# One batch's attention interleaved by priority, and VectorE's small steps with PSUM operands or an accumulator

## The chip, the cores and the metric

The kernel runs on one core of one Trainium2 chip. The metric is the time of one execution on the device in microseconds (us), the median over several runs. TensorE (PE) multiplies, PEld is its loading of weights, DVE is VectorE, ACT is ScalarE, POOL is GpSimd; SP issues the transfers. Each engine takes its own queue of instructions in order; an instruction may wait for semaphores of the others.

## The reference

Eight batches of S = 576 tokens. Three layers follow one another.

```python
a = exp(phi - phi.max(2)); a = a / (a.sum(2) + 1e-9)          # over the tokens, M = 32 memory slots
k_m = einsum('bhsm,bhsd->bhmd', a, k); v_m = einsum('bhsm,bhsd->bhmd', a, v)
x = softmax(q @ k_m.T / 8) @ v_m                               # 8 heads of 64: x is 576 x 512
u = x + (x.T @ U @ V).T                                        # rank 32, over the tokens
y = u + relu(u @ w_ch1) @ w_ch2                                # 512 -> 2048 -> 512
# then four experts, the two with the largest logits y @ w_gate kept for each token:
p = softmax(causal(y @ wq[e] @ (y @ wk[e]).T / 8)); out += w[e] * (p @ (y @ wv[e])) @ wo[e]
```

## The kernel before, in words

Every product is made from halves: a float32 operand is scaled by a power of two and split into a high and a low float16 part, and three matmuls (high·high, high·low, low·high) replace one in float32. The power of two comes from the largest absolute value of the operand. That largest value lies in one column, a number for each partition; to spread it over all partitions, `diagonals` (L236 to L242) writes a diagonal matrix of it (bfloat16, identity times the column, L241, tile `dg`, for the large weights `dgw`), `over_rows` (L244) multiplies that by ones on TensorE into a PSUM tile, a reduction on VectorE takes the maximum of each row, and `scales` (L253 to L259) makes the two powers of two from it with three steps on VectorE.

`stage1(b)` is the attention to the memory and the rank-32 mix. It reads phi and the raw q, k, v in four pairs of heads. For each pair: `pair_max` (absolute maxima; for batch 1 on ScalarE, L598), `pair_scale` (L612 and `scales`), `pair_hl` (splits to `kvq`, the low halves on GpSimd, L636, or VectorE, L639), `pair_kv` (36 matmuls `kv`, L656), `pair_kb`, `pair_scores` (18 matmuls `ss`, L683 to L685, and the transposition `vt`), then the softmax: `soft_a` (L783, L785) and `soft_b` (sum L795, then L797, the reciprocal L799, and the multiplication on GpSimd at L804 into `at`). For two pairs together `half_t` (transposing DMA to `aT`), `half_p` (`tu`, L826), `half_tt` (`tt`, L834), `half_tx` (`tx`, L846) and `half_u` (`u`, L873, L878) follow, then `u_max`, `u_scale` and `u_split` (`uhl`, L973, L975).

`mlp(b)` is 768 matmuls in four rounds: 8 `up` of 12 matmuls (`up`, L999; ScalarE L1003 and VectorE L1005 split the result to `h`) and 4 `down` in two parts of 12 (`dn`, L1015; VectorE adds into `u` at L1022). `stage2(b)` is the experts: `y_split` (L1093, L1095), `proj` (`pj`), `vg`, `gate`, `unit_s` (scores `sc` and softmax, `pT` by a transposing DMA), `unit_v` (`av` in PSUM, L1299), `unit_o` (L1306: denominators on ScalarE; L1308 reciprocal, L1310 times the gate's weight into `fac`; then ScalarE L1335 scales `av` to `ohl`) and `unit_w` (`wo`, output).

The first part of the program, `run(True)`, holds the conversion of w1 and w2 (`w1_conv`, `w2_conv`, `w1_split`, `w2_split`; L266 to L326; long steps of 128x1024 elements on ScalarE, VectorE and GpSimd), stage 1 of batch 0, the MLP of batch 0 and stage 1 of batch 1. The second, the loop, holds for b = 1 to 6 the MLP of b, stage 2 of b−1 and stage 1 of b+1. The last part takes the MLP of batch 7 and two stage 2 in an order written out by hand (`ORDER2`).

The order of the instructions: `at(t, step)` puts a step at a time in units, `run` traces the steps by that time, and a scheduler then orders each engine's queue by the trace order as priority, by its own estimate of when operands are ready. In the first part, the instructions of a step with `fill=True` are moreover held behind the last instruction, on each engine, of the recorded steps with a time up to the step's own less a slack; steps without it are recorded. PSUM has eight banks: tags `m` (3), `a` (4) and `v` (1, the `av` of the loop).

Of the kernel before, what the change touches and what calls it, by code (L numbers as in the profile page):

```python
# [46 lines left out]
START, SLACK, SLACK2, LATER = 53, 1.5, 4, 8  # L47
# [1509 lines left out]
```

## Time and profile before

| | |
|---|---|
| median of 3 runs | 1375.76 us (1375.38 to 1377.32) |
| the profiled execution | 1374.29 us, its span 1372.2 us |
| PE busy | 1240.5 us, 90% of the span |
| DVE busy | 962.7 us, 70% |
| ACT busy | 785.1 us, 57% |
| POOL busy | 406.7 us, 30% |
| granted TensorE clock, mean | 0.966 of full speed |

The numbers below PE are shares over the whole span; the stages have different limits, and the rows further down cut the span at the joints of the stages. The span leaves out 2.09 us of the execution's time. The loop from about 245 to 1270 us is three quarters of the span.

### The profile page before, as it was taken

What the parts mean: (1) busy time and instruction counts of PE and PEld (TensorE: products, weight loads), DVE (VectorE), ACT (ScalarE), POOL (GpSimd) and SP (SyncE); (2) the same over time, 40 slices, a digit from 0 to 9 for tenths busy, and PEclk for the clock granted to TensorE, in tenths of its full rate; (3) what the DMA queues carried; (4) which work ended last, traced back from release to release, by engine and by line L of the source; (5) the groups of instructions that cost most, each with busy time, mean ns of one, the idle gap of its engine ahead of it and who ended that gap; (6) DMA issues with size and microseconds to landing.
All of it is one profiled execution on the core that took longest, in us unless ns stands there. A gap on an engine that the chain in (4) does not pass through costs nothing. (4 is left out here: it accounts for less than half of the span.)

```text
span 1372.2 us, 31039 instructions
## 1 busy us (share of the span) xinstructions
PE 1240.5 (90%) x11932; PEld 950.0 (69%) x11932; DVE 962.7 (70%) x2673; ACT 785.1 (57%) x1886; POOL 406.7 (30%) x379
## 2 busy tenths in 40 slices
PE   5676895999989999989999999998998999999987
PEld 4454683777767777767767677676777777787764
DVE  7799866886678676776676766777667765644565
ACT  3786633666556555655564574565556556534476
POOL 3656512242321322232331322333222223001121
PEclk9789996999999999999999999999999999999998
DMA  9753320053422433143422433234232322201235
GB/s 255 207 171 93 82 66 18 20 109 63 94 53 54 95 76 71 38 96 72 79 62 52 86 70 73 57 75 96 50 75 57 79 58 53 58 14 35 41 81 112
DMA packets 257156, 106.40 MB, mean 78 GB/s; under 512 B 203792, under 2 KB 248528, under 8 KB 257008
## 3 DMA queue, kind: packets, MB, share of 16 engines
q1 hardware_dynamic: 257008, 104.43, 33.9%
q8 instruction: 93, 1.52, 0.4%
q14 instruction: 55, 0.45, 0.1%
HBM read 52.21 MB, written 9.44 MB: 45 GB/s over the span
## 5 line engine op out<-in xcount | busy, mean ns | idle before, releaser
L999 PE MATMUL up<-uhl,w1s 128*128 128x288 f16 x3072 | 429.6, 293 | 41.7 <-DVE h L1005 36.3
L1015 PE MATMUL dn<-h,w2s 128*128 128x288 f16 x3072 | 411.4, 287 | 6.4 <-DVE h L1005 4.3
L999 PEld LDWEIGHTS <-w1s 128*128 128x128 f16 x3072 | 301.2, 100 | 144.7 <-issue 60.9
L1015 PEld LDWEIGHTS <-w2s 128*128 128x128 f16 x3072 | 294.7, 98 | 86.8 <-issue 7.5
L1238 POOL TENSOR_TENSOR phl<-pr,phl 128x128 f16<-128x128 f32 (+3 forms) x112 | 92.5, 826 | 323.5 <-ACT phl L1236 235.3
L1005 DVE SCALAR_TENSOR_TENSOR h<-up,h 128x288 f16<-128x288 f32 x256 | 113.0, 450 | 84.0 <-ACT h L1003 83.1
L1003 ACT ACTIVATE h<-up 128x288 f16<-128x288 f32 x256 | 100.5, 401 | 87.7 <-PE up L999 85.4
L1235 ACT ACTIVATE pr<-sc,nm 128x128 f32<-128x128 f32 (+3 forms) x112 | 58.7, 524 | 122.3 <-DVE nm L1229 66.2
L636 POOL TENSOR_TENSOR kvq<-raw,kvq 96x768 f16<-96x768 f32 x48 | 78.4, 1652 | 145.9 <-ACT raw L630 139.8
L600 DVE TENSOR_REDUCE amax<-raw 96x1 f32<-96x768 f32 x72 | 68.1, 946 | 68.1 <-DMA raw<-in_v_dram 31.7
L1022 DVE SCALAR_TENSOR_TENSOR u<-dn,us,u 128x288 f32<-128x288 f32 x128 | 65.1, 509 | 33.0 <-PE dn L1015 32.4
L1299 PE MATMUL av<-vhl,pT 128*128 128x64 f16 (+1 forms) x1260 | 68.2, 195 | 14.7 <-DMA pT<-phl 13.3
L1299 PEld LDWEIGHTS <-pT 128*128 128x128 f16 (+1 forms) x1260 | 56.6, 102 | 35.7 <-DMA pT<-phl 17.9
L1229 DVE CUSTOM_DVE_ANT_0 sc<-sc,wmask,ysc 128x128 f32<-128x128 f32 (+3 forms) x128 | 69.3, 550 | 11.9 <-PE sc L1226 10.9
L624 ACT ACTIVATE kvq<-raw,ps 96x768 f16<-96x768 f32 x72 | 62.5, 924 | 6.6 <-DVE ps L257 6.5
L1236 ACT ACTIVATE phl<-pr 128x128 f16<-128x128 f32 (+3 forms) x112 | 52.2, 466 | 13.9 <-DMA pT<-phl 12.0
L1335 ACT ACTIVATE ohl<-av,fac 128x64 f16<-128x64 f32 (+1 forms) x140 | 35.7, 307 | 42.3 <-PE av L1299 33.2
L1356 PE MATMUL wo<-wos,oT 128*128 128x512 f16 (+1 forms) x288 | 57.0, 347 | 1.2 <-ACT oT L1328 0.7
L1153 PE MATMUL vg<-wvg,yhl 128*128 128x260 f16 (+1 forms) x504 | 49.2, 256 | 0.0
L1105 PE MATMUL pj<-yhl,wqs 128*128 128x288 f16 x336 | 47.4, 290 | 0.7 <-ACT u L881 0.7
L1120 ACT ACTIVATE qst<-pj 64x288 f16<-64x288 f32 x56 | 22.6, 404 | 42.7 <-PE pj L1105 42.3
L1105 PE MATMUL pj<-yhl,wks 128*128 128x288 f16 x336 | 46.6, 286 | 0.0
(317 smaller groups left out, 2291.2 us busy)
## 6 DMA issues: line engine op xcount, KB each, us to landing
w1s<-in_moe_w_ch_dram SPq DMA_DIRECT2D x32, 256.0 KB, 4.3
w2r<-in_moe_w_ch_dram SPq DMA_DIRECT2D x8, 1024.0 KB, 5.3
out_dram<-ob SPq DMA_DIRECT2D x28, 256.0 KB, 2.1
raw<-in_k_dram SPq DMA_DIRECT2D x48, 144.0 KB, 2.6
raw<-in_v_dram SPq DMA_DIRECT2D x48, 144.0 KB, 2.9
raw<-in_q_dram SPq DMA_DIRECT2D x48, 144.0 KB, 2.6
phi<-in_phi_dram SPq DMA_DIRECT2D x16, 288.0 KB, 3.6
rx<-in_k_dram SPq DMA_DIRECT2D x16, 144.0 KB, 4.1
```

The costliest lines, as they stand in the source:

```text
L600: dve.tensor_reduce(o, raw, axis=AX.XYZ, op=ALU.max, apply_absolute_value=True)
L624: act.activation(hl[:, 0], src, AF.Copy, scale=s[0:SP, j:j + 1])
L636: pool.tensor_tensor(hl[:, 1], src, hl[:, 0], op=ALU.subtract)
L999: pe.matmul(pm, w1s[:, f // 2, a, kc, f % 2 * P:f % 2 * P + P], uhl[c][:, kc], start=(n == 0), stop=(n == 3 * KC - 1))
L1003: act.activation(hb[:, 0, g], pm, AF.Relu)
L1005: dve.scalar_tensor_tensor(hb[:, 1, g], pm, 0.0, hb[:, 0, g], op0=ALU.max, op1=ALU.subtract)
L1015: pe.matmul(pm, w2s[:, m, fg, a, g], hb[:, c, g], start=(g == 0 and a + c == 0), stop=(g == FG - 1 and a == 1))
L1022: dve.scalar_tensor_tensor(y, pm, st["us", b][:, 4 + KC * fg + m:5 + KC * fg + m], y, op0=ALU.mult, op1=ALU.add)
L1105: pe.matmul(pp[:, 0:NH], w[:, a, kc, ep * P:(ep + 1) * P], yhl[:, c, kc, ts_], start=(n == 0), stop=(n == 3 * KC - 1))
L1229: dve.tensor_tensor_reduce(psc[:, 0:n], psc[:, 0:n], wmask[:, (NT - 2 - i) * P:(NT - 1) * P], cs, 3.0e38, ALU.add, ALU.min, nm)
L1238: (dve if tail and TD >> (2*i + eo) & 1 else pool).tensor_tensor(phl[:, n:2 * n], pr[:, 0:n], phl[:, 0:n], op=ALU.subtract)
L1299: pe.matmul(pav[:n, eo * D:(eo + 1) * D], lhs, vhl[:kn, c, j, vs], start=(j == 0 and a + c == 0), stop=(j == i and a == 1))
```

## The change

Three things are changed. Stage 1 of batch 1, with its `u_scale` and `u_split`, is neither held behind recorded steps nor recorded (`fill=None`), and its times are 6 units earlier (`LATER` 8 to 2; `u_scale` at 55.5 instead of 61 after the MLP's start). Of the odd chunks of w2 the first three conversions are put 9, 6 and 7 us of the plan earlier, the last load 2 earlier. VectorE's small steps get another form: the diagonals also write a sum that nobody reads (`dsum`); the maximum of the rows is written into PSUM beside the rows (`largest`), and `scales` works from there; `soft_b` keeps its sum in the scores' PSUM tile; the reciprocal of `unit_o` goes into two columns of the `av` tile's bank.

```diff
-START, SLACK, SLACK2, LATER = 53, 1.5, 4, 8
+START, SLACK, SLACK2, LATER = 53, 1.5, 4, 2
...
-            dve.tensor_scalar(d[:n_, j, 0:n_], identb[:n_, :n_], cols[:, j:j + 1], None, op0=ALU.mult)
+            dve.tensor_scalar(d[:n_, j, 0:n_], identb[:n_, :n_], cols[:, j:j + 1], 0.0, op0=ALU.mult, op1=ALU.add, accum_out=dsum[:n_, j:j + 1])
...
-        t = ps_a(name).rearrange("p (w n) -> p w n", n=P)[:, 0:w, 0:n_]
-        pe.matmul(t, onesb[:n_], d[:n_, 0:w, 0:n_], start=True, stop=True)
-        return t
+        t = ps_a(name)
+        rows = t.rearrange("p (w n) -> p w n", n=P)[:, 0:w, 0:n_]
+        pe.matmul(rows, onesb[:n_], d[:n_, 0:w, 0:n_], start=True, stop=True)
+        return rows, t[:, 3 * P:3 * P + w]
+
+    def largest(rows):
+
+        rows, beside = rows
+        dve.tensor_reduce(beside, rows, axis=AX.X, op=ALU.max)
+        return beside
...
-        dve.tensor_scalar(t, mx, down, 1e-30, op0=ALU.mult, op1=ALU.max)
+        dve.tensor_scalar(mx, mx, down, 1e-30, op0=ALU.mult, op1=ALU.max)
         yield 0.1
-        dve.tensor_scalar(s.bitcast(I32), t.bitcast(I32), 0x7F800000, 0x7F800000,
+        dve.tensor_scalar(s.bitcast(I32), mx.bitcast(I32), 0x7F800000, 0x7F800000,
                           op0=ALU.bitwise_and, op1=ALU.bitwise_xor)
-        dve.tensor_scalar(t.bitcast(I32), t.bitcast(I32), 0x7F800000, None, op0=ALU.bitwise_and)
+        dve.tensor_scalar(t.bitcast(I32), mx.bitcast(I32), 0x7F800000, None, op0=ALU.bitwise_and)
...
+            sb["pss", p] = psc[:SP, C * 64:C * 64 + G].rearrange("p (g o) -> p g o", o=1)
...
-            dve.tensor_reduce(sm, x, axis=AX.X, op=ALU.add)
+            ps_ = sb.pop(("pss", p))
+            dve.tensor_reduce(ps_, x, axis=AX.X, op=ALU.add)
             yield 0.1
-            dve.tensor_scalar(sm, sm, EPS, 1.0 / 32.0 if b else 1.0, op0=ALU.add, op1=ALU.mult)
+            dve.tensor_scalar(ps_, ps_, EPS, 1.0 / 32.0 if b else 1.0, op0=ALU.add, op1=ALU.mult)
             yield 0.1
-            dve.reciprocal(sm, sm)
+            dve.reciprocal(sm, ps_)
...
+            pav = values(i, ep)
...
-            dve.reciprocal(f[:n], f[:n])
+            fp = pav[:n, 2 * D:2 * D + 2]
+            dve.reciprocal(fp, f[:n])
             yield 0.1
-            dve.tensor_tensor(f[:n], f[:n], s2["wgt", b][:n, i, 2 * ep:2 * ep + 2], op=ALU.mult)
+            dve.tensor_tensor(f[:n], fp, s2["wgt", b][:n, i, 2 * ep:2 * ep + 2], op=ALU.mult)
...
-            if pin and not fill:
+            if pin and fill is False:
...
-        at((51, 57, 62, 78)[c] / UNIT, w2_load, 2 * c + 1)
-        at((73, 77, 86, 92)[c] / UNIT, w2_conv, 2 * c + 1, fill=True)
+        at((51, 57, 62, 76)[c] / UNIT, w2_load, 2 * c + 1)
+        at((64, 71, 79, 92)[c] / UNIT, w2_conv, 2 * c + 1, fill=True)
...
-        at(T0 + LATER + t, f, *a, fill=True)
-    at(T0 + 61, u_scale, 1, fill=True)
-    at(T0 + 62, u_split, 1, 0, fill=True)
+        at(T0 + LATER + t, f, *a, fill=None)
+    at(T0 + LATER + 53.5, u_scale, 1, fill=None)
+    at(T0 + LATER + 54.5, u_split, 1, 0, fill=None)
```

The remaining lines of the diff hand the tuple of `over_rows` to `largest` at its callers (`w1_scale`, `w2_conv`, `sw_scale`, `pair_scale`, `u_scale`, `y_scale`), drop the tiles that held the maximum before, and take the `av` tile through a helper, `values`, which both `unit_v` and `unit_o` call.

In TensorE's queue at the end of batch 0's MLP, this stood before (`ss_3` are the scores of batch 1's pair 3, `tu_1`, `tt_1`, `tx_1` its second half's mix, `u_2_0` its result; the MLP's last `dn` lies 109 rows, pair 3's `kv` and scores with their weight loads, ahead):

```order
L685 LDWEIGHTS qT
L685 MATMUL ss_3_2136<-kb,qT 96x64
L826 MATMUL tu_1_2223<-at,Uf 32x128 x6
L834 MATMUL tt_1_2235<-id_92,tt 128x32
L846 MATMUL tx_1_2257<-vtf,ttf 32x128 x2
L873 LDWEIGHTS vth
```

and now, with `dn_1_1_3` the last accumulation of the MLP:

```order
L1016 LDWEIGHTS w2s
L1016 MATMUL dn_1_1_3_2402<-h_1_8_2091,w2s 128x288
L838 MATMUL tt_1_2117<-id_93,tt 128x32
L850 MATMUL tx_1_2138<-vtf,ttf 32x128 x2
L877 LDWEIGHTS vth
```

The scores and `tu_1` have moved ahead of the last matmuls of the MLP (`tu_1` has 21 of them behind it), and `tt_1` now follows directly on the MLP.

In VectorE's queue at the same place stood before (`u_480` takes the MLP's sums, `kv_3` and `ss_3` are pair 3 of batch 1):

```order
L1025 TENSOR_REDUCE ym<-u_480 128x1
L795 TENSOR_REDUCE ssm<-sx 96x12
L1022 SCALAR_TENSOR_TENSOR u_480<-dn_1_1_3_2409,us,u_480 128x288
L797 TENSOR_SCALAR ssm<-ssm 96x12
L1025 TENSOR_REDUCE ym<-u_480 128x1
L799 RECIPROCAL ssm<-ssm 96x12
L1065 TENSOR_REDUCE ym<-ym 128x1
L668 TENSOR_TENSOR kf<-kv_3_2054,rm 128x64
L669 TENSOR_TENSOR vb<-kv_3_2054,rm 128x128
L672 CAST kb<-kf 128x64
L674 TENSOR_TENSOR kb<-kf,kb 128x64
L783 TENSOR_REDUCE smx<-ss_3_2136 96x12
```

and now, with `up_1_13` to `up_1_15` of the MLP's last round of `up`:

```order
L1006 SCALAR_TENSOR_TENSOR h_1_8_2091<-up_1_13_2225,h_1_8_2091 128x288
L670 TENSOR_TENSOR kf<-kv_3_1957,rm 128x64
L671 TENSOR_TENSOR vb<-kv_3_1957,rm 128x128
L1006 SCALAR_TENSOR_TENSOR h_1_8_2091<-up_1_14_2253,h_1_8_2091 128x288
L674 CAST kb<-kf 128x64
L676 TENSOR_TENSOR kb<-kf,kb 128x64
L1006 SCALAR_TENSOR_TENSOR h_1_8_2091<-up_1_15_2268,h_1_8_2091 128x288
L605 TENSOR_REDUCE amax<-raw_0_0_2624 96x1
L786 TENSOR_REDUCE smx<-ss_3_2028 96x12
L605 TENSOR_REDUCE amax<-raw_0_1_2629 96x1
L788 TENSOR_TENSOR sx<-ss_3_2028,smx 96x384
L1023 SCALAR_TENSOR_TENSOR u_481<-dn_1_1_0_2289,us,u_481 128x288
```

Pair 3's steps on `kv_3` (before: after the MLP's last sum) now stand among the splits `h` of the last quarter, and its softmax starts ahead of the last round's sums.

In VectorE's queue in the loop, at one tile of the experts, with what each instruction waits for, stood before:

```order
L785 TENSOR_TENSOR sx<-ss_2_4014,smx 96x384 [waits DVE_49,Pool_49]
L1022 SCALAR_TENSOR_TENSOR u_1731<-dn_1_0_0_4101,us,u_1731 128x288 [waits PE_49]
L1308 RECIPROCAL fac<-fac 128x2 [waits Activation_49]
L612 TENSOR_REDUCE ar<-ar_3_4144 128x3 [waits PE_49]
L1310 TENSOR_TENSOR fac<-fac,wgt 128x2 [waits DVE_49]
L795 TENSOR_REDUCE ssm<-sx 96x12 [waits Activation_49]
L255 TENSOR_SCALAR pi<-ar 128x3 [waits DVE_49]
L797 TENSOR_SCALAR ssm<-ssm 96x12 [waits DVE_49]
```

and now at another (`av_0_1` is the tile of values, which TensorE accumulates):

```order
L641 SCALAR_TENSOR_TENSOR kvq_4148<-raw_3_2_3981,ps,kvq_4148 96x6x64
L1023 SCALAR_TENSOR_TENSOR u_1623<-dn_1_0_2_4205,us,u_1623 128x288 [waits PE_49]
L1227 ISA sc_2_1_0_4249,nm<-sc_2_1_0_4249,wmask,ysc 128x384 [waits PE_49]
L1227 ISA nm 128x1
L1311 RECIPROCAL av_0_1_4105<-fac 128x2 [waits PE_49]
L1313 TENSOR_TENSOR fac<-av_0_1_4105,wgt 128x2 [waits DVE_49]
```

The reciprocal waited for ScalarE's sums before; now it waits for TensorE's last multiplication into the `av` tile, and the multiplication by the gate's weight follows it at once.

## Rows read from the trace of the kernel before

**Rows 1.** Windows: start:end, length, busy PE, PEld, DVE, ACT, POOL; PEclk, DMA, GB/s.

```profile
76.00:160.00 84.00, 61.52 (x499) 45.97 (x497) 81.56 (x140) 61.39 (x95) 55.28 (x27) 0.95 0.36 103
210.00:236.80 26.80, 10.62 (x89) 7.21 (x89) 13.32 (x43) 8.94 (x17) 6.91 (x6) 0.58 0.12 22
214.00:218.00 4.00, 2.78 (x45) 2.55 (x42) 0.75 (x4) 0.41 (x2) 2.16 (x2) 0.50 0.00 0
236.80:245.00 8.20, 7.39 (x41) 4.94 (x41) 8.20 (x21) 5.84 (x9) 0.03 (x1) 0.72 0.01 2
245.00:1270.00 1025.00, 978.08 (x9666) 757.56 (x9666) 709.65 (x2055) 579.50 (x1458) 278.48 (x276) 0.99 0.31 66
```

**Rows 2.** PE in order of time: start us, us, line, operation [idle before <-releaser].

```profile
205.49 4.45 PE L1015 MATMUL dn<-h,w2s 128*128 128x288 f16 x35
...
213.82 0.99 PE L656 MATMUL kv<-e,kvq 96*128 96x64 f16 x18 [3.69 <-POOL kvq L636]
...
222.91 1.07 PE L826 MATMUL tu<-at,Uf 96*32 96x128 f32 x12 [4.03 <-POOL at L804]
...
228.81 1.62 PE L873 MATMUL u<-aT,vth 128*128 128x288 f16 x6 [2.75 <-DMA aT<-ah]
...
236.76 0.88 PE L999 MATMUL up<-uhl,w1s 128*128 128x288 f16 x3 [0.62 <-ACT uhl L973]
```

**Rows 3.** What PE waited for, 76 to 160 us: total us, times, longest.

```profile
PE up L999 <- DVE h L1005: 7.7, 4, 3.6
PE w2mx L250 <- DVE dgw L241: 5.8, 2, 4.3
```

**Rows 4.** VectorE, then GpSimd, in order of time.

```profile
108.27 0.23 DVE L241 TENSOR_SCALAR dg<-identb,amax 96x96 bf16<-96x96 bf16 x1
...
114.70 3.90 DVE L241 TENSOR_SCALAR dgw<-identb,part 128x128 bf16<-128x128 bf16 x1
...
114.13 2.09 POOL L584 TENSOR_TENSOR e<-phi,e 96x768 f16<-96x768 f32 x1
116.19 2.36 POOL L287 TENSOR_TENSOR w2z<-w2z,w2r 128x1024 int32<-128x1024 int32 x1
```

**Rows 5.** VectorE, then GpSimd, beside a step that writes its accumulator.

```profile
88.46 1.20 DVE L279 TENSOR_SCALAR_CACHE_REDUCE w2s<-w2s 128x1024 f32<-128x1024 f32 x1
89.59 0.07 DVE L279 DVE_READ_ACCUMULATOR w2s<-w2s 128x1 f32 x1
...
88.24 2.41 POOL L287 TENSOR_TENSOR w2s<-w2s,w1s 128x1024 int32<-128x1024 int32 x1 [5.01 <-DVE t L255]
```

**Rows 6.** VectorE's groups by form, 76 to 160 us: xcount | busy, mean ns.

```profile
L241 DVE TENSOR_SCALAR dgw<-identb,part 128x128 bf16<-128x128 bf16 x6 | 8.2, 1366 | 0.8 <-ACT w2r L382 0.8
...
L241 DVE TENSOR_SCALAR dg<-identb,amax 96x96 bf16<-96x96 bf16 x9 | 5.9, 685 | 0.0
...
L255 DVE TENSOR_SCALAR pi<-ar 128x3 f32<-128x3 f32 x2 | 3.7, 1834 | 0.0
```

**Rows 7.** A group of ScalarE, 0 to 160 us; VectorE in order of time.

```profile
L598 ACT ACTIVATE junk<-rx 96x768 bf16<-96x768 f32 x9 | 7.5, 834 | 0.0
...
81.27 1.96 DVE L518 TENSOR_REDUCE pmx<-phi 96x256 f32<-96x768 f32 x2
```

**Rows 8.** Groups of VectorE by form, 245 to 1270 us.

```profile
L241 DVE TENSOR_SCALAR dg<-identb,amax 96x96 bf16<-96x96 bf16 x70 | 30.0, 435 | 0.5
...
L1310 DVE TENSOR_TENSOR fac<-fac,wgt 128x2 f32<-128x2 f32 x52 | 20.5, 394 | 0.7
...
L1308 DVE RECIPROCAL fac<-fac 128x2 f32<-128x2 f32 x52 | 8.2, 159 | 13.3 <-ACT fac L1306 13.1
```

**Rows 9.** What PE waited for, 245 to 1270 us; VectorE in order of time.

```profile
PE up L999 <- DVE h L1005: 28.6, 18, 3.5
PE av L1299 <- DMA pT<-phl: 13.3, 16, 2.0
...
1035.64 3.30 DVE L1095 SCALAR_TENSOR_TENSOR yhl<-u,ysc,yhl 128x288 f16<-128x288 f32 x5 [0.70 <-ACT yhl L1093]
```

More of the change, by code (lines that the diff above doesn't have):

```diff
@@ L205 @@
     dve.memset(amax, 0.0)
+    dsum = cpool.tile([P, 3], F32, name="dsum")
     one = cpool.tile([SP, 1], F32, name="one")
@@ L358, in w1_scale @@
         yield 0.3
-        dve.tensor_reduce(part[:, 0, o + 1:o + 2], rows, axis=AX.X, op=ALU.max)
-        yield from scales(part[:, 0, o + 1:o + 2], sw1[:, 2 * g:2 * g + 1], sw1[:, 2 * g + 1:2 * g + 2])
+        yield from scales(largest(rows), sw1[:, 2 * g:2 * g + 1], sw1[:, 2 * g + 1:2 * g + 2])
     def w1_split(c):
@@ L383, in w2_conv @@
             yield
-        mx = spool.tile([P, 1], F32, tag="mx", bufs=3, name="mx")
         d = diagonals(ps_, spool.tile([P, 1, P], BF16, tag="dgw", bufs=3, name="dgw"))
@@ L388, in w2_conv @@
         yield 0.3
-        dve.tensor_reduce(mx, rows, axis=AX.X, op=ALU.max)
-        yield from scales(mx, sw2[:, c:c + 1], t2[:, c % 2 * KC + c // 2:c % 2 * KC + c // 2 + 1],
+        yield from scales(largest(rows), sw2[:, c:c + 1], t2[:, c % 2 * KC + c // 2:c % 2 * KC + c // 2 + 1],
                           down=2.0 ** -13 if WM2 >> c & 1 else 0.5)
@@ L451, in sw_scale @@
         for o, r in zip((0, 3), rows):
-            dve.tensor_reduce(wmx[:, 8 + o:8 + o + r.shape[1]], r, axis=AX.X, op=ALU.max)
-        yield from scales(wmx[:, 8:13], wsc[:, 0:5], wt[:, 0:5])
+            n = r[1].shape[1]
+            yield from scales(largest(r), wsc[:, o:o + n], wt[:, o:o + n])
         yield
@@ L601, in pair_max @@
                 yield 0.5
-            ar = bpool.tile([P, 3], F32, tag="ar", bufs=4, name="ar")
             sb["arr", p] = over_rows(amax[0:SP, p, 0:3], f"ar{b}_{p}")
-            sb["ar", p] = ar
         def pair_scale(p):
@@ L611, in pair_scale @@
             sb["sc", p] = s
-            dve.tensor_reduce(sb["ar", p], sb.pop(("arr", p)), axis=AX.X, op=ALU.max)
-            yield from scales(sb.pop(("ar", p)), s, r, down=2.0 ** -13)
+            yield from scales(largest(sb.pop(("arr", p))), s, r, down=2.0 ** -13)
             yield 0.1
@@ L888, in u_max @@
             yield 0.2
-            ur = mpool.tile([P, 1], F32, tag="ur", name="ur")
-            st["ur", b] = ur, over_rows(um[:, KC:KC + 1], f"ur{b}")
+            st["ur", b] = over_rows(um[:, KC:KC + 1], f"ur{b}")
         if b == 0:
@@ L956, in u_scale @@
         st["us", b] = us
-        ur, rows = st.pop(("ur", b))
-        dve.tensor_reduce(ur, rows, axis=AX.X, op=ALU.max)
-        yield from scales(ur, us[:, 0:1], us[:, 2:3])
+        yield from scales(largest(st.pop(("ur", b))), us[:, 0:1], us[:, 2:3])
         yield
@@ L1065, in y_max @@
             dve.tensor_reduce(ym[:, 8:9], ym[:, 0:8], axis=AX.X, op=ALU.max)
-            yr = ap.tile([P, 1], F32, tag="yr", bufs=2, name="yr")
             yield 0.2
-            s2["yr"] = yr, over_rows(ym[:, 8:9], f"yr{b}")
+            s2["yr"] = over_rows(ym[:, 8:9], f"yr{b}")
         def y_scale():
@@ L1078, in y_scale @@
                 s2["yhl"] = ap.tile([P, 2, KC, S], F16, tag="yhl", name=f"yhl{b}")
-            yr, rows = s2.pop("yr")
-            dve.tensor_reduce(yr, rows, axis=AX.X, op=ALU.max)
-            yield from scales(yr, c[0], c[2])
+            yield from scales(largest(s2.pop("yr")), c[0], c[2])
             yield 0.1
@@ L1281, in unit_s_last, with values @@
                 s2["pT", i, ep, eo] = pT
+        def values(i, ep):
+            if ("av", i, ep) not in s2:
+                s2["av", i, ep] = ps_m(f"av{b}_{i}_{ep}", 512) if tail else ps_v(f"av{b}_{i}_{ep}")
+            return s2["av", i, ep]
         def unit_v(i, ep, eo):
@@ L1287, in unit_v @@
             n = TAIL if last else P
-            if ("av", i, ep) not in s2:
-                s2["av", i, ep] = ps_m(f"av{b}_{i}_{ep}", 512) if tail else ps_v(f"av{b}_{i}_{ep}")
-            pav = s2["av", i, ep]
+            pav = values(i, ep)
             e = 2 * ep + eo
@@ L1304, in unit_o @@
             ss = s2.pop(("ss", i, ep))
+            pav = values(i, ep)
             f = ap.tile([P, 2], F32, tag="fac", bufs=2, name="fac")
@@ L1307, in unit_o @@
             yield 0.2
-            dve.reciprocal(f[:n], f[:n])
+            fp = pav[:n, 2 * D:2 * D + 2]
+            dve.reciprocal(fp, f[:n])
             yield 0.1
-            dve.tensor_tensor(f[:n], f[:n], s2["wgt", b][:n, i, 2 * ep:2 * ep + 2], op=ALU.mult)
+            dve.tensor_tensor(f[:n], fp, s2["wgt", b][:n, i, 2 * ep:2 * ep + 2], op=ALU.mult)
             yield
-            pav = s2.pop(("av", i, ep))
             if tail:
```

## The prediction

> **What bounds the kernel now.** I read the page's shares first, then the span in stretches, then TensorE's time order where its share is low, then who releases it there. [rows 1] is the span in stretches that I cut at the kernel's own joints. In the long one, 245 to 1270 us, which is the loop over batches 1 to 6, PE is busy 978.08 of 1025 us: TensorE bounds it, and VectorE has 315 us to spare there. Two stretches are not bound by TensorE. From 76 to 160 us (batch 0's MLP beside the rest of the weight conversion and the beginning of batch 1's stage 1) VectorE is busy 81.56 of 84 us and PE only 61.52: VectorE bounds it, and PE idles 22.5 us. From 210 to 236.8 us PE is busy 10.62 of 26.8 us: nothing bounds it but a chain. [rows 2] shows that chain on PE: the last row of batch 0's MLP ends at 205.49 + 4.45 = 209.94, then come `kv`, the scores, `tu`, `u`, and batch 1's first `up` starts at 236.76. Three gaps (3.69 for GpSimd's `kvq`, 4.03 for GpSimd's `at`, 2.75 for the transposing DMA of `aT`) are waits for other engines. The granted clock is 0.50 from 214 to 218, the lower level, after PE had idled 3.69 us [rows 1, 2]. So 26.8 us lie between two MLPs with PE nearly empty, and no other stretch is like it.
>
> **The change, part by part.** The sum is made against the profiled execution, 1374.29 us, of which the span is 1372.2; the median of the runs is 1375.76, 1.47 above it, which I add at the end.
>
> *1. Batch 1's stage 1 by priority.* Its steps keep their order, but no instruction of it is held behind an MLP instruction any more, and its times are 6 units earlier. The order of the instructions is what counts: PE's queue has pair 3's `kv` before the last 110 to 150 matmuls of the MLP instead of behind them, its scores 80 before the end, and `tu` of the second half 21 before the end; `tt`, `tx` and `u` stay behind it. VectorE's queue has pair 3's `kb` among the `up` rows of the last quarter (the order of VectorE above). A `dn` matmul takes 4.45/35 = 0.127 us [rows 2], so `tu` is 21 × 0.127 = 2.7 us before the end. From `tu` to the first `up` it is 236.76 − 222.91 = 13.85 us in before; 2.7 of them are now covered, 11.1 remain, and the gap shrinks from 26.8 to 11.1: **−15.7, say −16**. Pair 3's soft steps took 4.0 us between scores and `tu`; there are 59 matmuls or 7.5 us between these now, so `tu` should not wait. What is late next is the chain that remains: `tt`, the `aT` transposition, `u`, its maximum and split, which nothing covers. Bounds: −17.3 if some 3 us of PE's work in the part left take half at the full clock; −5 if PE, which takes its queue in order, stands inside the MLP at `kv` or the scores for the same releasers as before (the gaps of [rows 2], 3.69 + 4.03 + some of the rest, move in with them).
> The moved PE work is not free: 36 + 18 matmuls and the transposition of `vt`. In the gap they lie between 213.82 and 218.88 (222.91 − 4.03), some 5 us at the lower clock with short waits in it, and at the full one take half or less: **+2** inside the MLP (0 to +4).
>
> *2. The start of batch 0's MLP.* ScalarE's queue now has three `pair_max` of batch 1 ahead of batch 0's `half_u`, 3 × 0.83 = 2.5 us [rows 7], and VectorE has phi's maxima, 1.96 us for two [rows 7], and two diagonals among the steps that give batch 0's scale. Batch 0's input chain runs through both engines. **+3**, between 0 (they fit in the gaps while the chain waits for PE) and +5 (all on it).
>
> *3. VectorE's small steps.* [rows 4] shows what they cost: a diagonal of 96×96 takes 0.23 us by itself, while the `dgw` diagonal that starts at 114.70 takes 3.90 and ends at 118.60, when GpSimd's second operation from there (116.19 + 2.36 = 118.55) ends. A step of some 0.23 us stood through two of GpSimd's. A form with accumulator ran at 88.46 in 1.20 us while GpSimd's L287 ran from 88.24 to 90.65 [rows 5]: it did not wait, and from this row I take that such waits go where the step has this form. That PSUM operands do the same (for `fac`, `scales`, `soft_b`) no row shows; I take it likewise, and price the other case as E. [...]
> In 76 to 160 us the excess over the undisturbed durations is 6 × (1.366 − 0.23) = 6.8 for `dgw`, 9 × (0.685 − 0.23) = 4.1 for the diagonals of `amax`, 2 × (1.834 − 0.16) = 3.3 for L255 [rows 6]: 14.2 us of VectorE, in a stretch which it bounds and in which PE waited 5.8 us for `dgw` and 7.7 for `h` behind it [rows 3]. Not all of it is PE's, since the conversion's long steps (1.2 us each) slide into the room, and two conversions come earlier (times 64, 71, 79 instead of 73, 77, 86), as do batch 1's steps. I take half: **−7** (bounds −14.2 and +3, if the earlier work eats it and the accumulator's read, 0.07 us each [rows 5], is added).
> In the loop: 70 × (0.435 − 0.23) = 14.4 us of diagonals and 52 × (0.394 − 0.16) = 12.2 of `fac` [rows 8], together 26.6 off VectorE, against some 80 accumulator reads × 0.07 = 5.6 on it. But VectorE has spare time there, and PE's waits, 28.6 us for `h` [rows 9], lie mostly behind rows of `y_split`, as at 1035.64, 3.30 us of L1095 [rows 9], which stay. **−3** (bounds −28.6, all these waits, and the price of the next point).
> *4. The reciprocal in `av`'s bank.* Before, `fac` was ready while PE still multiplied; now the reciprocal waits for the tile's own last `av` matmul (the order of VectorE above). After it come 0.16 us of reciprocal and 0.16 to 0.39 of multiplication before ScalarE can take `av` [rows 8]. There is one `av` bank in the loop, but the 65 tiles of the loop's 1025 us stand 15.8 us apart on average, so the next one's matmuls are seldom due: I cost this at **0**; without that cover it is 0.16 + 0.16 and two hand-overs, some 0.45 us for each of 65 tiles in the loop, +29. VectorE's next rows stand behind the waiting reciprocal, `h` among them, and PE waits for `h`. The Trainium skill speaks against the step here (PSUM — Partial Sum Buffer, section PSUM bank collisions raise a hardware error): PSUM is to be guarded by bank, not by address, so the reciprocal may not go beside the matmuls in other columns. No trace here shows it but the wait in the order agrees; by that rule this point is rival C.
> *5. The clock.* PE is at the lower level from 214 [rows 1]. A shorter gap would leave less of that, but from 236.8 to 245 VectorE is busy 8.20 of 8.20 us [rows 1], with the splits of the small weights before `h`, and PE is held by that: 0. What follows the loop has the last 15 of the 80 tiles of point 4: 0 ± 3.
>
> **Sum**: −16 + 2 + 3 − 7 − 3 = −21. 1374.29 − 21 = 1353.3; for the median 1353.3 + 1.5 = 1354.8, **1355 us**.
>
> **Rivals.**
> *B. The stall moves in instead of going.* PE's queue is in order, and `kv` of pair 0 now stands after 200 of 768 matmuls, where VectorE and GpSimd are still busy with the conversion (55.28 of 84 us on GpSimd [rows 1]). For it: VectorE bounds just that stretch, and more of batch 1 is put into it. Against: the waits of point 3 leave it. Then the stretch from 76 to 160 takes +3 in place of −7, the start its upper bound of +5, and the loop gives nothing: −16 + 2 + 5 + 3 = −6, 1370.
> *C. Slower: the reciprocal's wait decides.* Each of the 65 tiles costs 0.45 us on the path: −21 + 29 = +8, 1384. The point from which it decides is 21/65 = 0.32 us a tile, just the two operations without hand-overs. For it: VectorE's queue is in order and `h` stands behind; PE waits 13.3 us for `pT` before `av` already [rows 9], so `av`'s last matmul is often late. Against: the 315 us that VectorE has to spare in the loop.
> *D. The loop gains as well.* If half of the 28.6 us of waits for `h` goes with the 26.6 us of VectorE's: −14 in place of −3, 1344.
> *E. The change does not do what it says* (the new forms wait for GpSimd all the same): both terms of point 3 fall, −21 + 7 + 3 = −11, 1365; this lies between A and B.
>
> **How the numbers follow.** A (1355) 0.58, B with E (1365 to 1370) 0.20, D (1344) 0.11, C (1384) 0.11. The measurement can tell 0.2%, 2.75 us, from no change. A's own range is 1348 to 1362. Leaving C and the far end of D out, the range is 1342 to 1374. Faster: A, D and nearly all of B, 0.86; same: the slow end of B and the fast end of C, 0.03 + 0.02; slower: the rest of C, 0.09.
>
> **What would show it.** After batch 0's last `dn`, PE's time order shows `tt` at once and the next `up` some 11 us later; a gap above 18 us refutes point 1. In the MLP of batch 0, `kv` and `ss` stand with waits under 1 us; waits of 3 us there speak for B. The groups of L242 have means near 0.24 us, and GpSimd's operations beside them 2.4 us; else E. In the loop, PE busy stays at 978 and the stretch shrinks by 3; if PE's waits for `h` grow, or `av` waits for ScalarE, it is C. The forecast is wrong above all if the part that moves in finds VectorE with no room.

## The result, and the profile after

The changed kernel takes 1365.08 us (median of 4 runs, 1360.92 to 1368.24) against 1375.57 us before: ratio 0.9909, 95% interval 0.9887 to 0.9931. It is faster by 10.5 us, half of what was forecast. Beside the experiments, in another session, it had 0.9894 (0.9864 to 0.9925).

The profiled execution after is the longest of its four (1368.24 us, span 1366.3), that of before, 1374.29, is below all four of before, so the two spans differ by 5.9 us only. The stages, cut by the starts of the first and the last matmul of each MLP in TensorE's order of time (us; "loop" is from batch 1's first matmul to batch 7's last, "rest" what follows):

| | first `up` of batch 0 | batch 0's MLP | gap | loop | rest | span |
|---|---|---|---|---|---|---|
| before | 71.8 | 137.9 | 27.1 | 1069.1 | 66.3 | 1372.2 |
| after | 76.0 | 145.5 | 10.8 | 1067.2 | 66.8 | 1366.3 |
| after, second execution | 77.6 | 144.3 | 10.7 | 1066.5 | 65.1 | 1364.2 |

The gap fell by 16.3 us; batch 0's MLP, which was to shorten by 5, got 7.6 longer (6.4 in the second execution). TensorE after, in order of time, from the end of that MLP to the next:

```profile
211.16 7.39 PE L1016 MATMUL dn<-h,w2s 128*128 128x288 f16 x59
218.49 0.64 PE L830 MATMUL tu<-at,Uf 96*32 96x128 f32 x12
219.06 2.75 PE L1016 MATMUL dn<-h,w2s 128*128 128x288 f16 x21
221.64 0.31 PE L838 MATMUL tt<-id,tt 96*128 96x32 f32 x2
222.64 0.41 PE L850 MATMUL tx<-vtf,ttf 128*32 128x128 f32 x4 [0.69 <-DVE ttf L841]
...
225.71 0.69 PE L882 MATMUL u<-V,txs 96*128 96x288 f32 x3 [1.81 <-DVE txs L858]
...
229.22 0.29 PE L252 MATMUL ur<-dg,onesb 128*128 128x128 bf16 x1 [2.33 <-DVE dg L242]
...
232.30 0.88 PE L1000 MATMUL up<-uhl,w1s 128*128 128x288 f16 x3
```

These answer to [rows 2]: `tu` stands in the `dn` matmuls without a wait, `tt` follows the last of them at once, and the first `up` comes 10.7 us after `tt` begins. What PE waited for inside batch 0's MLP, 76 to 220 us (total, times, longest), against [rows 3]:

```profile
PE ss L685 <- DVE kb L674: 6.0, 2, 5.2
PE up L1000 <- DVE h L1006: 4.2, 4, 1.5
PE w2mx L252 <- DVE dgw L242: 3.2, 1, 3.2
PE dn L1016 <- DVE u L1023: 2.4, 1, 2.4
PE dn L1016 <- DVE h L1006: 2.0, 1, 2.0
```

`up`'s waits for `h` and the wait for `dgw` are 7.4 us together, where they were 13.5 in [rows 3], a shorter stretch, but a wait for `kb` of 5.2 us is new. What that makes in all, as in [rows 1]: batch 0's MLP, then its first 96 matmuls, an eighth of it, before:

```profile
71.79:209.94 138.15, 115.10 (x992) 87.69 (x991) 117.66 (x225) 84.68 (x140) 66.87 (x34) 0.94 0.38 103
71.79:90.99 19.20, 15.05 (x100) 10.69 (x100) 19.20 (x32) 13.84 (x20) 9.24 (x3) 0.85 0.67 196
```

and after:

```profile
75.97:221.80 145.83, 121.66 (x1055) 91.91 (x1054) 117.96 (x245) 86.59 (x141) 73.42 (x40) 0.92 0.34 90
75.97:105.50 29.53, 18.87 (x112) 12.41 (x112) 28.18 (x47) 25.98 (x36) 19.21 (x8) 0.82 0.44 129
```

TensorE's idle time in this MLP rose by 1.1 us only (138.15 − 115.10 = 23.05, then 24.17), its busy time by 6.6: some 2.6 are matmuls that moved in, 4.0 the MLP's own 768 (`up` and `dn`, 106.5 us, then 110.5), at a mean granted clock of 0.92 in place of 0.94. And the first eighth alone takes 10.3 us longer. There VectorE was busy all the time before and is busy 28.18 of 29.53 us now. It is not the old waits: the `dgw` of this MLP (76 to 222 us) against [rows 6] are

```profile
L242 DVE TENSOR_SCALAR_CACHE_REDUCE dgw<-identb,part 128x128 bf16<-128x128 bf16 x6 | 2.0, 335 | 0.6 <-ACT w2r L389 0.6
```

The groups of VectorE, 240 to 1262 us, that answer to [rows 8]:

```profile
L242 DVE TENSOR_SCALAR_CACHE_REDUCE dg<-identb,amax 96x96 bf16<-96x96 bf16 x70 | 20.8, 302 | 0.6
L1311 DVE RECIPROCAL av<-fac 128x2 f32<-128x2 f32 x51 | 8.4, 165 | 9.5 <-PE av L1300 8.3 <-ACT phl L1234 0.7
L1313 DVE TENSOR_TENSOR fac<-av,wgt 128x2 f32<-128x2 f32 x51 | 7.9, 154 | 2.1 <-PE av L1300 1.5
L242 DVE DVE_READ_ACCUMULATOR dg<-identb,amax 96x1 f32 x70 | 5.5, 79 | 0.0
```

The multiplication fell from 394 to 154 ns: its waits are gone. So are those of the diagonals, but their new form takes 302 ns and 79 for reading the accumulator, 381 in all, where the old one had a mean of 435 with its waits and 230 without. PE's waits for `h` in the loop, against [rows 9] (240 to 1265 us):

```profile
PE up L1000 <- DVE h L1006: 18.3, 13, 2.8
PE av L1300 <- DMA pT<-phl: 12.6, 19, 1.5
PE pj L1103 <- ACT u L885: 4.9, 3, 1.6
```

The waits for `h` fell by 10 us, others rose (`pj` 0.7 to 4.9), and the loop is 2 us shorter, which is within the 3 us by which the loop of one kernel differs between two executions (below).

The new 5.2 us, in order of time on TensorE:

```profile
162.25 0.26 PE L685 MATMUL ss<-kb,qT 128*96 128x64 f16 x1 [5.17 <-DVE kb L674]
```

on VectorE, before that:

```profile
157.38 0.28 DVE L671 TENSOR_TENSOR vb<-kv,rm 128x128 f32<-128x128 f32 x1
157.58 4.52 DVE L674 CAST kb<-kf 128x64 f16<-128x64 f32 x1
162.14 0.22 DVE L676 TENSOR_TENSOR kb<-kf,kb 128x64 f16<-128x64 f32 x1
```

and on GpSimd meanwhile:

```profile
154.72 3.17 POOL L328 TENSOR_SCALAR w2z<-w2z,sw 128x1024 f32<-128x1024 f32 x2
157.85 4.19 POOL L330 TENSOR_TENSOR w2s<-w2z,w2s 128x1024 f16<-128x1024 f32 x2
```

The cast of a 128x64 tile, 0.18 us in the loop's mean, starts while GpSimd works and ends at 162.10, when GpSimd's second operation from there ends (157.85 + 4.19 = 162.04). This is a wait as in [rows 4], on a step whose form the change left alone, and TensorE's queue now has the scores that need it inside the MLP. The granted clock is at its lower level (0.5) behind that wait, as the rows beside the experiment with kf show.

### The profile page after: what moved, and what is told of

Read it like the earlier page. It is cut to its first block, busy times and chain, and to the rows that moved or that the text cites. A ratio compares the mean times of both kernels' runs of the same rounds, so it can differ in the third digit from the quotient of the medians.

```text
span 1366.3 us, 31204 instructions
## 1 busy us (share of the span) xinstructions
PE 1242.5 (91%) x11932; PEld 950.9 (70%) x11932; DVE 938.0 (69%) x2791; ACT 786.8 (58%) x1886; POOL 409.2 (30%) x379
## 5 line engine op out<-in xcount | busy, mean ns | idle before, releaser
L1300 PE MATMUL av<-vhl,pT 128*128 128x64 f16 (+1 forms) x1260 | 68.7, 195 | 14.2 <-DMA pT<-phl 12.6
L1234 ACT ACTIVATE phl<-pr 128x128 f16<-128x128 f32 (+3 forms) x112 | 52.3, 467 | 15.3 <-DMA pT<-phl 13.2
L1337 ACT ACTIVATE ohl<-av,fac 128x64 f16<-128x64 f32 (+1 forms) x140 | 35.7, 307 | 41.9 <-DVE fac L1313 21.7
L1103 PEld LDWEIGHTS <-wqs 128*128 128x128 f16 x384 | 38.0, 101 | 17.8 <-issue 6.8
```

What stands on the lines that cost most here:

```text
L1103: pe.matmul(pp[:, 0:NH], w[:, a, kc, ep * P:(ep + 1) * P], yhl[:, c, kc, ts_], start=(n == 0), stop=(n == 3 * KC - 1))
L1300: pe.matmul(pav[:n, eo * D:(eo + 1) * D], lhs, vhl[:kn, c, j, vs], start=(j == 0 and a + c == 0), stop=(j == i and a == 1))
```

## The experiments

Every ratio is to the kernel before in the same session, with its 95% interval. The stages of all profiled executions, cut as above:

| | first `up` | MLP 0 | gap | loop | rest | ratio |
|---|---|---|---|---|---|---|
| changed kernel again | 77.6 | 144.3 | 10.7 | 1066.5 | 65.1 | 0.9894 (0.9864 to 0.9925) |
| forms only | 74.7 | 134.6 | 28.3 | 1067.1 | 65.0 | 0.9967 (0.9945 to 0.9990) |
| placing only | 77.3 | 144.7 | 12.7 | 1071.4 | 64.8 | 0.9990 (0.9969 to 1.0012) |
| kf in PSUM | 78.7 | 139.7 | 10.8 | 1067.0 | 68.0 | 0.9896 (0.9868 to 0.9924) |
| dsum apart | 74.2 | 137.9 | 11.7 | 1064.9 | 64.7 | 0.9846 (0.9814 to 0.9878) |
| dsum apart, kf in PSUM | 73.9 | 142.0 | 13.1 | 1065.3 | 64.0 | 0.9892 (0.9861 to 0.9922) |
| the same, phi pinned | 74.7 | 146.6 | 13.6 | 1066.8 | 64.6 | 0.9937 (0.9913 to 0.9961) |
| fac in SBUF | 77.8 | 144.5 | 10.8 | 1062.5 | 65.9 | 0.9898 (0.9861 to 0.9935) |
| dsum apart again | 77.1 | 141.0 | 12.2 | 1062.2 | 64.7 | 0.9870 (0.9843 to 0.9896) |
| forms only, dsum apart | 73.7 | 131.4 | 28.7 | 1065.2 | 66.8 | 0.9896 (0.9877 to 0.9915) |
| dsum apart, w2 as before | 75.1 | 141.9 | 11.0 | 1061.5 | 65.0 | 0.9853 (0.9833 to 0.9873) |
| old diagonals | 75.7 | 139.9 | 11.9 | 1074.1 | 66.4 | 0.9956 (0.9938 to 0.9973) |

One kernel's stages differ between two executions by up to 3 us (dsum apart), the loop by 3.

Batch 0's MLP in eighths, 96 of its 768 matmuls each (us, from the start of the first to the start of the next eighth's first, in the last one to the start of its last):

| | 1 | 2 | 3 | 4 | 5 | 6 | 7 | 8 |
|---|---|---|---|---|---|---|---|---|
| before | 19.2 | 14.8 | 27.0 | 16.2 | 19.0 | 13.2 | 14.7 | 13.8 |
| after | 29.5 | 16.0 | 21.1 | 13.1 | 21.7 | 15.1 | 15.8 | 13.2 |
| changed kernel again | 29.5 | 13.4 | 22.6 | 13.2 | 21.6 | 15.1 | 15.6 | 13.2 |
| forms only | 19.3 | 13.6 | 26.7 | 19.6 | 13.6 | 13.2 | 14.8 | 13.7 |
| placing only | 27.8 | 14.9 | 23.7 | 13.6 | 16.4 | 21.5 | 13.1 | 13.6 |
| kf in PSUM | 29.5 | 13.3 | 21.1 | 13.2 | 17.1 | 15.8 | 16.4 | 13.2 |
| dsum apart | 27.4 | 13.8 | 23.7 | 14.2 | 16.2 | 15.1 | 14.4 | 13.0 |
| dsum apart again | 27.4 | 13.7 | 24.3 | 14.2 | 19.0 | 15.1 | 14.1 | 13.0 |
| dsum apart, kf in PSUM | 27.5 | 13.7 | 24.3 | 12.9 | 18.3 | 17.7 | 14.1 | 13.6 |
| the same, phi pinned | 21.3 | 18.8 | 24.6 | 15.8 | 16.7 | 22.8 | 13.4 | 13.0 |

**The changed kernel again**, no edit.

> The changed kernel once more, unaltered, beside the others: ratio to before 0.991 (0.989 to 0.993). If the part of batch 0's MLP that got longer (7.7 us in the first profile) is a property of the instruction order, its first and last matmul of that MLP stand at 76 and 222 us again, within 2 us; if it came from one execution's lower clock, the MLP is shorter by 5 us or more here.

The long MLP is there again, 77.6 to 221.9 us: it belongs to the order, not to one execution.

**The forms alone**: the changed kernel with `LATER` 8, `fill=True` and the old times of `u_scale`, `u_split` and w2.

> Only VectorE's small steps have their new form; batch 1's stage 1 and the w2 conversion stand as before. Theory (the waits for GpSimd go from the small steps, but the long steps and the casts that still read and write SBUF in the two-port forms take over some of them): the gap between the two MLPs stays at 26 to 28 us, batch 0's MLP shortens by 3 to 7 us, the loop by 0 to 3: ratio 0.995, about 1369. Rival 1 (the forms bring nearly all of the gain of the whole change): 0.991 or less. Rival 2 (the reciprocal in av's bank costs as much as the waits give): 1.000 or more.

The MLP is 3.3 us shorter, the loop 2.0, the gap stays, and the start is 2.9 later: 0.9967, with an interval that holds the theory's 0.995 and the number of neither rival.

**The placing alone**: the kernel before with

```diff
-        at(T0 + LATER + t, f, *a, fill=True)
+        at(T0 + LATER + t, f, *a, fill=None)
```

with `LATER` 2 and the two steps on u placed as in the change.

> Only the placing of batch 1's stage 1 is changed; the forms and the w2 conversion are those of before. Theory: the gap falls from 26.8 to 11 to 14 us, and batch 0's MLP, from its first to its last matmul 138 us before, gets longer by 8 to 12 us, start later by 2 to 4: ratio 0.997 to 1.000. Rival (the longer MLP in the changed kernel comes from the forms or from w2): the MLP stays within 3 us of 138, ratio 0.989.

The gap falls by 14.4 and the MLP grows by 6.8, the start by 5.5: next to nothing is left, 0.9990. With the forms (−3.3) that would be an MLP 3.5 us longer; the changed kernel's is 6.4 to 7.6. The first eighth is 8.6 us longer with the placing alone and 0.1 with the forms alone: it comes from the placing. The 12 matmuls `es` of batch 1's phi, in the third eighth before, stand in this one now, 9 of them with the placing alone, and the third is shorter.

**kf in PSUM**, in the changed kernel:

```diff
-            kf = bpool.tile([P, 64], F32, tag="kf", bufs=2, name="kf")
+            kf = pk[:, 128:192]
```

> The changed kernel with one more step out of SBUF: the product kf of pair_kb is kept in PSUM beside kv, so that the cast to kb and its remainder read PSUM. In the changed kernel that cast took 4.52 us at 157.6 us beside GpSimd, and PE stood 5.17 us before the scores for it. Theory (the cast waited for GpSimd as the diagonals had): the cast takes under 0.3 us, the stall of PE before ss falls under 1 us, batch 0's MLP is 4 to 5 us shorter than in the changed kernel: ratio 0.987 to 0.988. Rival (the next step in the queue takes the wait, PE gets nothing): the cast is short but ratio stays at 0.991.

VectorE at the same place:

```profile
157.90 0.21 DVE L674 CAST kb<-kv 128x64 f16<-128x64 f32 x1
158.15 0.23 DVE L676 TENSOR_TENSOR kb<-kv,kb 128x64 f16<-128x64 f32 x1
```

and GpSimd beside it:

```profile
158.05 4.21 POOL L330 TENSOR_TENSOR w2s<-w2z,w2s 128x1024 f16<-128x1024 f32 x2
```

The cast takes 0.21 us beside the same operations of GpSimd, and PE's wait for it falls from 5.2 to 0.9: that the cast had waited because it went from SBUF to SBUF is shown. The Trainium skill (SBUF — State Buffer, section Who interferes with whom) counts a cast among the steps that can take the ports shared with GpSimd, and a step with at most one SBUF input outside those modes as free of them; both rows agree. But the wait did not go; the next step in VectorE's queue that works in SBUF has it, as the rival said. In the changed kernel again, then here:

```profile
162.94 0.69 DVE L289 TENSOR_SCALAR w2z<-w2z 128x1024 uint32<-128x1024 uint32 x1
158.31 4.50 DVE L289 TENSOR_SCALAR w2z<-w2z 128x1024 uint32<-128x1024 uint32 x1
```

and here TensorE stands behind that one:

```profile
163.29 6.20 PE L1000 MATMUL up<-uhl,w1s 128*128 128x288 f16 x48 [2.34 <-DVE u L1023]
```

So 5.2 us of waiting became 0.9 + 2.3, and other waits grew. As in [rows 1], six microseconds behind the wait and the whole MLP, in the changed kernel again:

```profile
162.00:168.00 6.00, 5.09 (x34) 3.87 (x35) 5.08 (x9) 1.48 (x4) 3.39 (x3) 0.50 0.00 0
77.56:222.14 144.58, 120.97 (x1055) 91.80 (x1054) 116.17 (x245) 86.89 (x141) 71.94 (x40) 0.92 0.35 90
```

and here:

```profile
162.00:168.00 6.00, 4.71 (x38) 3.62 (x38) 5.39 (x11) 1.97 (x5) 3.40 (x4) 1.00 0.00 0
78.71:218.70 139.99, 116.68 (x1055) 89.28 (x1054) 114.80 (x245) 86.19 (x141) 71.97 (x40) 0.96 0.35 93
```

The MLP is 4.6 us shorter than in the changed kernel of the same session, 4.5 of it in the fifth eighth, but TensorE's idle time in it is the same (23.6 and 23.3 us). The difference is busy time at another granted clock: behind the wait of 5.2 us it was at its lower level in all three executions that have this wait (the changed kernel's two and fac in SBUF), and behind the two shorter ones it was not. In the time the gain is not seen (0.9896 and 0.9894, both intervals 0.6% wide), though they can't rule out the theory's 0.987 to 0.988 either: the start and the rest of this execution were 1 and 3 us later.

**dsum apart**, in the changed kernel:

```diff
-    dsum = cpool.tile([P, 3], F32, name="dsum")
+    dsum = cpool.tile([P, 6], F32, name="dsum")
...
+        o = 0 if d is None else 3
...
-accum_out=dsum[:n_, j:j + 1])
+accum_out=dsum[:n_, o + j:o + j + 1])
```

> The changed kernel with dsum, the sum that nobody reads, split in two: three columns for the diagonals dg, three for the large weights' dgw. In the changed kernel and in the one with the forms alone, the diagonal of batch 0's largest u stands in VectorE's queue directly behind a dgw, and runs 4.2 us after its operand is there; in before it ran 0.2 us after. Theory (both write dsum's first column, so the scheduler must keep them in the order of the program, and the dgw waits for the conversion): the first matmul of batch 0's MLP comes 3 to 5 us earlier (72 to 74 us instead of 76 to 78), ratio 0.986 to 0.988. Rival (the delay comes from batch 1's phi and maxima in the same queues): no change at the start, 0.990.

VectorE from batch 0's largest u to its diagonal, in the changed kernel:

```profile
67.86 0.16 DVE L891 TENSOR_REDUCE um<-um 128x1 f32<-128x4 f32 x1
...
69.43 2.15 DVE L334 SCALAR_TENSOR_TENSOR w2s<-w2z,sw,w2s 128x1024 f16<-128x1024 f32 x1 [1.28 <-ACT w2s L332]
71.71 0.35 DVE L242 TENSOR_SCALAR_CACHE_REDUCE dgw<-identb,part 128x128 bf16<-128x128 bf16 x1
...
72.10 0.35 DVE L242 TENSOR_SCALAR_CACHE_REDUCE dg<-identb,um 128x128 bf16<-128x128 bf16 x1
```

and with dsum apart:

```profile
68.63 0.16 DVE L892 TENSOR_REDUCE um<-um 128x1 f32<-128x4 f32 x1
...
68.85 0.34 DVE L243 TENSOR_SCALAR_CACHE_REDUCE dg<-identb,um 128x128 bf16<-128x128 bf16 x1
```

In the changed kernel the diagonal stands behind a `dgw` and runs 4.24 us after the maximum, here 0.22. From that maximum to the first `up` it is 8.1 us in the changed kernel (67.86 to 75.97; 8.1 in the second execution, 69.43 to 77.56), and 5.6 here (68.63 to 74.23; 5.6 in the second, 71.54 to 77.13); before it was 5.1. The maximum itself comes at 66.7 to 71.5 us in the executions, for the same kernel at 68.6 and 71.5, so the absolute time that I had expected was no good measure. The ratio is 0.9846, more than the 2.5 us of the start explain. The eighths show more of it: against the changed kernel again the first is 2.1 us shorter and the fifth 5.4, since with this order PE's longest wait for `kb` is 0.3 us.

**dsum apart and kf in PSUM.**

> The changed kernel with dsum apart and kf in PSUM, both. Theory (two separate causes, one at the start, one inside the MLP): the first matmul at 72 to 74 us, no wait over 1.5 us for kb before the scores; batch 1's MLP starts 6 to 8 us earlier than in the changed kernel, at 225 to 227: ratio 0.983 to 0.986. Rival (what is saved at the start is waited for again inside, since VectorE bounds the first half): batch 1's MLP starts at 230 or later, 0.988 or more.

The two gains do not add: with dsum apart PE's longest wait for `kb` was down to 0.3 us already, so there was nothing left for kf to take. The rival's ratio (0.988 or more) came, and batch 1's MLP starts at 229.0, between its 230 and the theory's 227. That it came out slower than dsum apart (0.9892) I cannot assign; its MLP is 1 to 4 us longer.

**phi pinned**: as the last, and

```diff
-        at(T0 + LATER + t, f, *a, fill=None)
+        front = f.__name__ in ('phi_max', 'phi_sub', 'phi_split', 'phi_pes', 'phi_rm')
+        at(T0 + (8 if front else LATER) + t, f, *a, fill=True if front else None)
```

> As the one before, and of batch 1's stage 1 the five steps on phi (maximum, subtraction, split, sum, reciprocal) stand where they were before the change, held behind the MLP's instructions; the pairs stay by priority. Theory (in the first round of up ScalarE and VectorE do phi's work ahead of h: from matmul 36 to 96 the changed kernel took 17 us, before 10): that part takes 12 us or less, and batch 1's MLP starts another 2 to 4 us earlier: ratio 0.981 to 0.984. Rival (the phi work is only moved into the next round): the same as the one before within 0.002.

The part named took 11.9 us, as the theory had it, but the MLP as a whole 146.6, and PE waited 12.2 us for `h` in it. The first eighth is 6.2 us shorter than without the pinning, and the second and the sixth are 5.1 longer each: what leaves one part is paid in others, and more. The theory fell, and 0.9937 is also worse than the rival had it (0.9892 within 0.002).

**fac in SBUF**, in the changed kernel:

```diff
-            fp = pav[:n, 2 * D:2 * D + 2]
-            dve.reciprocal(fp, f[:n])
+            dve.reciprocal(f[:n], f[:n])
```

> The changed kernel with unit_o's reciprocal back in SBUF: fac is formed without waiting for av. Theory (the reciprocal in av's bank costs nothing in the loop, since the next tile's av comes much later): the loop from batch 1's first matmul to batch 7's last takes the same within 3 us (1067 us in the changed kernel), ratio 0.990 plus or minus 0.002. Rival C of the prediction (the wait costs 0.3 us or more for each of 65 tiles): the loop is 15 us shorter or more, 0.979. Third possibility (the multiplication's wait for GpSimd comes back and counts): the loop is 5 us longer, 0.994.

The multiplication's mean is back at 408 ns, the loop is 4 us shorter in this profile (1062.5), one more than the theory allowed, and the ratio the same, 0.9898. That is 4/65 = 0.06 us a tile for the wait for `av`, 0.1 if the 3 us between two executions are added, not 0.3: rival C is refuted.

**dsum apart again**, no further edit.

> The changed kernel with dsum apart once more, unaltered, since the version that moved the cast to PSUM as well came out slower than this one. Theory: the ratio 0.985 is a property of its order, 0.984 to 0.988 again, batch 1's MLP starts at 222 to 225 us. If it was chance of one session: 0.989 to 0.991.

0.9870 (0.9843 to 0.9896), median 1358.57 us after 1357.95: the gain repeats within the theory's range, but less of it against before, and the interval overlaps both of the changed kernel and reaches the rival's 0.989. Batch 1's MLP starts at 230.3, outside what I expected, 3 of the 6.5 us to the first execution by its start. Nearly all the rest is the fifth eighth, first here in the earlier execution, then in this one (as in [rows 1]):

```profile
153.30:169.60 16.30, 12.84 (x111) 9.73 (x110) 11.12 (x18) 7.61 (x16) 14.58 (x8) 1.00 0.10 23
156.80:175.80 19.00, 15.55 (x110) 10.84 (x108) 11.18 (x18) 7.51 (x16) 14.52 (x8) 0.82 0.11 24
```

TensorE is idle 3.5 us in both; the same matmuls take 2.7 us longer at a granted clock of 0.82 than at 1.00.

**The forms alone, with dsum apart.**

> The forms alone (stage 1 and w2 as before), with dsum apart. The forms alone had 0.997, a first matmul at 74.7 us and a gap of 28.3. Theory (dsum delays the start of batch 0's MLP also without the new placing): the first matmul at 71.5 to 73, the gap unchanged, ratio 0.994 to 0.995. Rival (the delay needs batch 1's steps in the queue): 74 to 75, 0.997.

The first matmul comes at 73.7, just above the theory's bound, but 5.0 us after the maximum (68.65), against 7.1 in the forms alone (67.56 to 74.70). The ratio is 0.9896 against 0.9967, more than the 0.994 to 0.995 expected: here, too, the shared dsum cost more than the start shows; the MLP is 3.2 us shorter and the loop 1.9. And this version, without the new placing, can't be told from the whole changed kernel (0.9909 and 0.9894): with dsum apart the placing and w2 add 0.3 to 0.5% (0.9870 and 0.9846), with intervals that overlap or touch.

**dsum apart, w2 as before.**

> The changed kernel with dsum apart and the conversion of w2 at its old times. Theory (the earlier conversion adds to a stretch which VectorE bounds and takes from one that PE bounds, so it is worth little): batch 1's MLP starts within 3 us of 224, ratio 0.984 to 0.988. Rival (the earlier w2 is what lets the last down run on): batch 1's MLP starts 5 us later or more, 0.989.

0.9853: the earlier conversion of w2 is worth nothing that can be measured; batch 1's MLP starts at 228.0, a microsecond outside the theory's 3, but between the two executions with the new times (223.8 and 230.3).

**The old diagonals**, in the changed kernel, without the sum.

> The changed kernel with the diagonals in their old form, without the sum; all other small steps as changed. Theory (two effects of opposite sign: the old form waits for GpSimd, some 10 us of VectorE before 160 us; the shared dsum is gone, 4 us at the start): the diagonals of dgw have a mean over 0.6 us in batch 0's MLP, the first matmul comes at 72 to 75 us, batch 0's MLP is longer than the 138 us of the version with dsum apart by 4 us or more: ratio 0.988 to 0.991. Rival (the accumulator form is worth nothing but its new wait costs): 0.985, as with dsum apart.

The waits are back; the groups of VectorE between 66 and 236 us:

```profile
L242 DVE TENSOR_SCALAR dg<-identb,amax 96x96 bf16<-96x96 bf16 x14 | 6.4, 490 | 0.0
L242 DVE TENSOR_SCALAR dgw<-identb,part 128x128 bf16<-128x128 bf16 x7 | 4.7, 666 | 3.6 <-ACT w2r L389 3.6
```

Batch 0's MLP is no longer than with dsum apart (139.9 us against 137.9 and 141.0; no dsum is written), so the 4 us that I expected there are not seen. But the loop is 1074.1 us, 7 longer than in the changed kernel, and the ratio 0.9956, beyond what either side expected. So the new form of the diagonals is worth some 0.5%, and this one profile puts it into the loop. It is not VectorE's time, though; its group there, 240 to 1262 us, is

```profile
L242 DVE TENSOR_SCALAR dg<-identb,amax 96x96 bf16<-96x96 bf16 x70 | 25.3, 367 | 0.5
```

25.3 us, where the new form takes 20.8 and 5.5. PE's waits for `h` are longer (23.1 us, the longest 5.2, against 18.3 and 2.8). Why they are stays open.

## Why the prediction was right, and where it was off

The direction, the gap and the range were right (1365 in 1342 to 1374), the size was half: the number lies between A and B. That it is just the number of rival E is chance, since the new forms do not wait as E has it. By its steps:

- **The gap, −16**: −16.3. Read from the right rows: 21 matmuls over `tu`, 11 us left.
- **The moved work and the start, +2 and +3**: the moved matmuls cost some 2.6 us inside the MLP, and the start is 4.2 to 5.8 later. Of that 3.0 us lie between the maximum of u and the first `up`, and 2.5 of these are the shared dsum, which I had overlooked: it makes the scheduler keep unrelated diagonals in the order of the program. ScalarE's maxima, which I had named, are not needed for it. With the placing alone, where no dsum exists, the start is 5.5 later, 1.3 of it after the maximum (70.93 to 77.34, before 66.72 to 71.79), and 4.2 before it; how much of that is the placing and how much the spread of the maximum's time stays open.
- **Point 3, −7 in batch 0's MLP: this is the step that failed.** I put half of 14.2 us of VectorE's waits to TensorE's account and bounded the other side at +3. Without the 2.6 us of moved matmuls it came out at +5.0 (+3.5 in the second execution, where they are 2.9), beyond that bound. The waits of the small steps did go: the `dgw` of batch 0's MLP have a mean of 335 ns and 79 for the accumulator, where [rows 6] has 1366, and the forms alone shorten this MLP by 3.3. But the time that they freed was taken: with batch 1's steps in it VectorE is busy 118.0 us in this MLP, and it was 117.7 before. The placing alone makes the MLP 6.8 longer, and the eighths show where: 8.6 us in the first (10.3 in the changed kernel), into which batch 1's work on phi moved, while the third and fourth are shorter (by 5.9 and 3.1 in the changed kernel). Pinning phi back only moved the cost. To this comes the cast to `kb`, still from SBUF to SBUF, which took 4.5 us beside GpSimd while TensorE stood for it; its eighth is 2.7 us longer than before, and the clock fell behind it. This is rival B, and the sign that I named for it came (a wait of 3 us or more at `ss`: 5.2). I gave it 0.20, with E, and looked for the stall at GpSimd's `kvq` and at `kv`, where it is 0.5 us; it is one step further, on VectorE. Its −6 meets the spans (−5.9) with some luck: the profiled execution is the longest of four, the second one's span is 8.0 below, and the parts are other than B's (the start +4.2 for +5, the MLP +7.6 for +5, the loop −1.9 for 0).
- **The loop, −3**: −1.9 and −2.6 in two executions. The sum behind it was off: the diagonals free 70 × (0.435 − 0.381) = 3.8 us, not 14.4, because their new form is itself longer, and yet the old ones in the changed kernel make the loop 7 us longer, which VectorE's time does not explain.
- **The reciprocal, 0**: right within 4 us, the loop's difference with fac in SBUF.
- **The clock, 0**: no experiment changes it alone. It was looked for behind the gap only, and the row named for the zero does not bear it: from 236.8 to 245 PE is busy 7.39 of 8.20 us at 0.72 [rows 1], so VectorE hardly holds it. Inside batch 0's MLP, where nothing was put down for it, the mean fell from 0.94 to 0.92, an estimated 3 us (0.06 × 138 us lost before, 0.08 × 146 after).
- **The level**: the sum was made against an execution that is faster than all four of the kernel before in the result; the medians differ by 10.5 us where the profiled executions differ by 5.9.

What stays open: why dsum apart gives more than the 2.1 to 2.5 us that the chain at the start shows (0.9894 to 0.9846 and 0.9870, 3 to 7 us; with the forms alone 0.9967 to 0.9896, 10 us). In the profiled executions part of it is the long wait for `kb`, which that order does not have, and the clock behind it. But with the old times of w2 a wait of 3.9 us for `kb` is there again and the ratio stays (0.9853), so this is not settled; with the forms alone nothing is assigned. Each edit also reorders a part of the queues, so a ratio here does not price one cause by itself. The version with dsum apart beats the kernel before clearly, and the changed one in the medians (1357.95 and 1358.57 us in two sessions, against 1365.08 and 1366.66 in two others), but the intervals of the ratios overlap in three of the four pairs. For a learner: taking a wait off VectorE pays only where nothing that waits behind it fills the room, so look at what stands next in the queue.
